# A threshold attention with a maxout feed-forward: the hand-written order of all engines, its PSUM slots and its masks written anew

## The chip, the core and the metric

The kernel runs on one core of one Trainium2 chip. The metric is device time in microseconds (us), from the runs of the whole program. Inputs and output are float32 in the chip's main memory. The engines are named as in the profile: PE (matmul), PEld (its weight loads), DVE (VectorE), ACT (ScalarE), POOL (GpSimd) and SP (SyncE, which here only issues DMAs).

## The reference

```python
# q, k, v: 8 batches x 8 heads x 576 rows x 64;  tau = 0.02
scores = (q @ k.T) / 8
thresh = max(scores, axis=-1) - tau
scores = where(scores >= thresh, scores, -1e9)
attn = exp(scores - max(scores)); attn /= sum(attn) + 1e-9
x = (attn @ v), heads side by side        # 4608 x 512
h = maximum(maximum(x @ w1, x @ w2), x @ w3)   # 512 -> 768
out = h @ w_out                           # 768 -> 512
```

Of each row of scores only the entries within tau of the row's maximum take part in the softmax. The feed-forward works on the rows of one batch, all eight heads together.

## The kernel before, in words

**Attention.** Four heads of a batch make a quad: 16 quads. A quad is worked in 9 chunks, and a chunk in 2 halves, so there are 144 chunks and 288 halves; a half is a score tile of 128 rows x 576 columns (`scores`, line 324). q and k come in as float32, are turned on PE (`transposed`, 293), copied out of PSUM, and q is also copied with its two partition halves exchanged (`swapped`, 277).

**The softmax of a half** has four forms. `MASKED` (line 24) holds one digit for each of the 288 halves and picks the form:

- 0: DVE writes the negated scores from PSUM into a buffer z with the row's extreme (`maximum`, 364); DVE makes the threshold, a small instruction (`threshold`, 375); ACT applies a Prelu to z (`exponents`, 379), then an Exp with a running sum (`numerators`, 388).
- 1: the same DVE pass; ACT applies one Exp to z; DVE then keeps the entries above exp(-tau) and sums them, in one SCALAR_TENSOR_TENSOR that reads z twice (`numerators`). No threshold.
- 2: as 0, but ACT's Prelu reads the scores in PSUM, and no threshold instruction is needed.
- 3: as 1, but ACT's Exp reads the scores in PSUM.

So 0 and 2 take two big ACT instructions and one big DVE one; 1 and 3 take one big ACT and two big DVE. A z buffer is held from the DVE pass until POOL has made the normalised bfloat16 P of that half (`normalized`, 400). There are 9 z buffers (`ZBUFS`, 34); from half 72 on, two more are borrowed (`half_of_z`, 357). When a chunk's P is complete, SP issues a transposing DMA (`turned`, 409), and when all 9 chunks of a quad have landed, two products with v can run (`product`, 415).

**Feed-forward.** For each batch, 18 pieces (6 slices of the hidden width by 3 weights) go through `hid` (490), then two output pieces (`outp`, 526) and a leftover (`ninth`). A piece is cut into two halves (`halves`, 457): the second half adds to the same PSUM as the first from the other half of the rows, so it is gated by a wait on the last matmul of the first half. Batch 7 is split in two parts whose pieces have no halves.

**PSUM.** There are four slots, 0 to 3, of 128 x 1024 float32 each (`bank`, 182). Every PE piece takes the slot whose number is written behind its letter, and has to wait until the piece that used it before has been read out.

**What sets the order.** Nothing is planned at run time. `ORDER` (line 40) is one long text, and the loop at line 789 issues one step for each letter. Each engine runs its own steps in the order in which the text has them (`_Ordered`, 84), and waits for the others by semaphores. The letters, by engine:

- PE: T turn q or k, S scores of a half, O product with v, F first half (or whole) of a feed-forward piece, B its second half, N leftover rows. T, S, O, F and N are followed by the slot.
- DVE: m maximum, s threshold, k masked numerators with sum, r reciprocal of a chunk's sums, c copy of k out of PSUM, w product out of PSUM, v maximum with a feed-forward piece, f the last output.
- ACT: a copy of q out of PSUM, e first exponent step, n Exp with sum, x product out of PSUM, h first of three feed-forward pieces, u output, j leftover rows.
- POOL: p normalise a half, q exchange halves of q, y cast of v, z cast of a weight.
- SP: l a load of q, k or v, g a load of a weight, t transposing DMA, o and i stores. The letter d is the very last output's store, which ACT's queue issues.

The profile puts nearly all instructions on line 93, the helper that every engine's call goes through. They are told apart by tiles: `sc` scores, `z` or `stage` softmax buffers, `P` normalised, `ptq` turned P, `o` product, `xt` feed-forward input, `ph` hidden pieces, `hm`/`hT` their maxima, `po` output in PSUM, `ob` output in SBUF, `tp` turned q and k, `qt`/`kt`/`qs` their copies.

Of the kernel before, what the change touches and what calls it, by code (L numbers as in the profile page):

```python
# [45 lines left out]
nyrrsmyBepT1svS0hpcT2nS3zmaS1erpgsF2mntpsBmnS3yvF1etssT0myeBprS2cnpS3mnS0ympelF2epF3lmBnzslssvS0htBrqmeS2vpn
S1gF0sepmF3teqBmF2erssvpBtnBkphF0eS1vtS3znmF2nrBmqteS1rpvBnS3pmlnF0pmgeS1qsBsrhmS3pevS2npS1mF0npsO3ermpesmO2
zewepgsskBxtT3nF1vS2nklBarS0mlphS3mtepF2sS1rmnyBmetF3pvT0eBpcnS2tzT1nvS0asmzS3temS2qeS1meF0trkpmS3lenpBmnlys
reklpF1umerpskS3upBeoketmS0uS2umpS3tesmS1qeT0myO2nqlrsnlprcO3etqsmepwS0xptS1mnF3psnmS2BlerskpS1thF0meF3pmeBF
2ktnBveBsrS1nvpS0hmyF3emF2npBrssT0eprtvBaF1kS3nqvBeF0myhyS2kyleF3mBelBvnpS2snsS0vptemS1pnF3rmpT2tnBmpeF0scS1  # L50
htBrnmpF3erT2rpvlBasS1pstvnS2pmeF0pS3emtBqnmT2S1hcqS3empF2eS0rsqmtS1epsmBeF3pmnF0stsvBeBknF2klhF1BvelS0nrvpB
emT3pS2arvS0ptnS3mpnO1smtesrkpeF2swnlrpmeT0S1qtescS3epBmnpmnT0trskS3paS1umS0ulqmeS3lmyS1nopS2smelS0rmeS3psmn
O1ypersmqO2etkpemO0lewqxlknpS3tS1keF2momS3lexF0ktT1enkBercpnsBpumN1ertkphkF3jS0rursS1empBnmF2ptS0vpS1smeF3yt
BsnsmBpnvS0pT1hmF2atT3srepS0cF1eprBsmeqF3vnByBynvplS2nsS0plmhS1mteS2mF0nF3mteS1rrspBnmS2pelvBlepF1smT0leqBvl
aS2rkhF3oqnsS0mtS1epmBeqsF2ssmtS0epvBeyF1mnF3vpBesrS0ktphBermS1npT2svO0nytmpncT3eS1wF2nrmS0aBrsmnqF3vnT1pS0c
eBptsF2mhpS1eS3pmteS0qmBeO1spmnkteF3rvnpT0BsskapS2xvS0erS1qmtnS3pmnF2mqlespmeS1rtkBepresmT3puS1cuS0ptmnS3pS2
meyS1lrekpF0tnsmempO3lekteskO2nrsmpeBkpxrnwS1uptS3muS2pnmF0yoeS1mF3lesymBtnS2srkpS1hmBeF0spveF2ertBmpT3nrsvS
1paBlmpnS0tS3qhmF1epsmS2leBymF3tevF0nBknlS1rsvpS2esmqnBF3srmhpS1epS0tmeF2pssBrempBtesvS0ynF1mT3lnpBvF0lhsrcS
2tnT1mBnF3valS2nrBsqmeF0pvS1epS2meBptsmS3eqF1hmT2peBcS3tnskT2O0arkplnmO2lerpvewptS3xkpS1nF2meF0sstreBsmpS3nv
pBnmS1tS2hmT3eF0rmpnF1cBpnBrevptT3S2apvS0qmtS3S1enmqF2esrsqmiepmleS0soykeS1plBnmemtS3ukS0uT1snrlO2cpekynO1me  # L60
ymeF3pwxskteS0keS1BrrnkopmF2pmS0BqeuurtsmF1phS3srnpS2meT0ptBmeS3ykpaN2esvempF0tS1jkpF3ermBeS2ptvnS1pmBnS0rls
hsmpS2elF3mqntS1mpF0nsrBskpeF2lsmBetBpveF1yhvS3lnkS2lesF0mytnBmBerqsS3veF2lpvnF1pBsmT0htBceF3rT2vnpBsaS0pvnF
1qmtS2nBsrnmT0pS3hrcpF2esS1mpteS0rmpS3emBpntF1svqnS0ssBmpeoT2vO3lamtneF1wS0nrlBpmeS3qsrS2hsmS0pnmF1eptS3smeB
pmF2ntS0veS3rsmnpS1BnpO0veytrempS2empS3xsmS1tekF0nsknlT2rmpBelmlpnscS3quS1umyS2eorT0kpeO3tmeyO1ewlepsmF3etka
rknS2qklT0nBmxespcS2eryF0mpF1uskpuBtnS2BhmqF3nsvS0peS2srmtpF1eBmpeF0srvnBptS2hyS3pmeF1lmeBlBevtF3nkT2S0arrvp
BnS2mphS1smpF0ntS3smnpBmeF1lsT2esvlF3nrBrcptBnvpS2eS0qmlhS1tsnprsmT3F2epmS0aptBemF3yevS1oS0nqmBnpsrS2mnF1ptv
S0epmBeS3mthS2skeF0F1snmlBeklO3ersvpnrmByepF0swT2eqtBvnqF3ssrcS1hpiBmpT0S2vaptS1snmS0pnT3mqF2tecT1BarmS3pnS1
vqeS0mF2pesrmnptmS3npT1seS0qctBeymqermpS1eS3mpuF0nmtuskS1eS2klnS3smBesrsepO1upmemO2txrkpukeO3wnkpS0xS2emF3et
rmS1pnBssspmF2hS0rtepS3mnBpmF1etS0veF3mnN2rnpBpjF0evtF2esBkBkhF1nsvS3eBmBevO3hrkS2pwnS1mnF3prmS2eptsF0mnBpsS
1sevyS2terBmpeF3svS1iyepBmoS0yhmtF2ekF3nBsmS1ersBvpnF0pmeF2BvteS1hBmF3rsS0vpeF1rknpBBmnO2vhptO0xrpnS3pwS2trm  # L70
npS0mnF3pmteF1pBeBvtS0rS2vpS3empF1ktkF0kBereskpemBkperumO2uptO3xpN1wtenkO2jrF3pxF1hpF2nvF3tvF1rhF2pvF3pvF1hF
# [758 lines left out]
```

## Time and profile before

| | |
|---|---|
| median of 3 runs | 446.92 us (446.69 to 449.09) |
| profiled execution, span from first to last instruction | 444.8 us |
| what the runs' median has beyond that span | 2.1 us |
| PE busy | 422.4 us (95%) |
| ACT busy | 403.0 us (91%) |
| DVE busy | 392.8 us (88%) |
| POOL busy | 311.9 us (70%) |
| mean DMA traffic | 199 GB/s |

The page gives no time of its own for the profiled execution beside the span, so sums are made against the span, and the 2.1 us are added to compare with the runs. Busy shares are means over stages that differ: a head in which only attention of the first batch can run, a long middle in which attention and feed-forward of earlier batches interleave, and a tail with only the last batch's feed-forward. A busy PE counts matmuls whose ends are modelled, and weight loads have their own row.

### The profile page before, as it was taken

To read this page: it belongs to the slowest core of one execution; us is meant where nothing else is said; L and a number is where in the kernel's file an instruction comes from. 1 tells how busy PE (TensorE), PEld (TensorE's weight loads), DVE (VectorE), ACT (ScalarE), POOL (GpSimd) and SP (SyncE) were. 2 spreads that over 40 slices of the span, in tenths; PEclk is the share of its full clock that TensorE was granted. 3 is DMA by queue.
4 is the path that set the end of the run, shared out by engine and by line. 5 is a ranking of instruction groups with operands and counts; after the bars stand their busy time and mean duration, and the time that the engine had idled before them with its cause. 6 is when DMAs were issued, how large, how long until landed. Compare 5 with 4: busy or idle time off the path is not lost.

```text
span 444.8 us, 14254 instructions
## 1 busy us (share of the span) xinstructions
PE 422.4 (95%) x5188; PEld 320.2 (72%) x5190; DVE 392.8 (88%) x1228; ACT 403.0 (91%) x836; POOL 311.9 (70%) x420
## 2 busy tenths in 40 slices
PE   7767789999999999999999999999999999999996
PEld 6334347787788767787788777788688886787873
DVE  3887999999999999999999999998999998899642
ACT  3999999999999999999999999899999999987632
POOL 2799989997878687696785877676676685457400
PEclk8998999999999999999999999999999999999999
DMA  7999999999999999699899999989999977487633
GB/s 188 275 293 199 291 169 269 235 243 262 229 180 194 212 222 292 125 256 167 143 234 189 230 198 203 209 168 210 208 206 194 244 151 105 83 179 136 145 116 108
DMA packets 213959, 88.50 MB, mean 199 GB/s; under 512 B 189184, under 2 KB 202240, under 8 KB 213888
## 3 DMA queue, kind: packets, MB, share of 16 engines
q1 hardware_dynamic: 213360, 86.96, 95.9%
q8 instruction: 41, 0.67, 0.6%
q10 hardware_dynamic: 528, 0.62, 0.5%
q14 instruction: 30, 0.25, 0.2%
HBM read 35.65 MB, written 9.44 MB: 101 GB/s over the span
## 4 chain that ended last, share of the span: by engine, by line
PE 86%; ACT 5%; DVE 4%; issue 2%; DMA 1%; SPq 0%; DVEq 0%; ACTq 0%
PE ph L93 32%; PE sc L93 32%; PE po L93 10%; PE o L93 9%; ACT z L93 5%; PE tp L93 3%; DVE z L93 3%; DMA qm<-in_q_dram 1%; ACT qt L93 1%; SPq L93 0%; DVE xt L93 0%; DVE hm L93 0%; DVE stage L93 0%; DVE rs L93 0%; ACT ob L93 0%
## 5 line engine op out<-in xcount | busy, mean ns | idle before, releaser
L93 POOL TENSOR_SCALAR P<-z,rs 128x576 bf16<-128x576 f32 x250 | 200.6, 814 | 63.3 <-DVE rs L93 28.1
L93 DVE TENSOR_SCALAR_CACHE_REDUCE z<-sc 128x576 f32<-128x576 f32 x250 | 183.7, 750 | 14.8 <-PE sc L93 10.1
L93 PE MATMUL sc<-kt,qs 64*128 64x256 f32 (+2 forms) x640 | 182.6, 423 | 5.7 <-DVE z L93 2.3
L93 PE MATMUL sc<-kt,qt 64*128 64x320 f32 (+2 forms) x640 | 182.4, 433 | 5.2 <-ACT z L93 3.3
L93 PE MATMUL ph<-xt,w 64*128 64x288 bf16 (+2 forms) x2160 | 170.8, 283 | 0.1
L93 PEld LDWEIGHTS <-w 64*128 64x128 bf16 (+1 forms) x2160 | 130.1, 94 | 28.6 <-issue 4.3
L93 ACT ACTIVATE z<-z 128x576 f32<-128x576 f32 x174 | 117.6, 679 | 0.1
L93 PEld LDWEIGHTS sc<-kt,qs 64*128 64x128 f32 (+1 forms) x640 | 92.4, 180 | 25.7 <-DVE z L93 5.7
L93 ACT ACTIVATE z<-z,th 128x576 f32<-128x576 f32 x143 | 106.2, 769 | 5.0 <-DVE th L93 4.2
L93 PEld LDWEIGHTS sc<-kt,qt 64*128 64x128 f32 (+1 forms) x640 | 91.9, 179 | 19.7 <-ACT z L93 5.9
L93 DVE SCALAR_TENSOR_TENSOR z<-z 128x576 f32<-128x576 f32 x76 | 62.2, 830 | 0.5 <-ACT z L93 0.5
L93 PE MATMUL po<-wo,hT 64*128 64x512 bf16 (+3 forms) x454 | 53.5, 354 | 0.3
L93 POOL COPY qs<-qt 64x640 f32<-64x640 f32 (+3 forms) x66 | 43.0, 652 | 10.8 <-ACT qt L93 7.2
L93 ACT ACTIVATE z<-z,nm 128x576 f32<-128x576 f32 x68 | 50.6, 767 | 0.0
L93 DVE TENSOR_TENSOR hm<-ph,hm 128x576 bf16<-128x576 f32 (+2 forms) x54 | 37.0, 686 | 9.2 <-PE ph L93 8.9
L93 ACT ACTIVATE hm<-ph 128x576 bf16<-128x576 f32 (+2 forms) x54 | 31.8, 589 | 13.4 <-PE ph L93 12.8
L93 POOL TENSOR_SCALAR P<-stage,rs 128x576 bf16<-128x576 f32 x38 | 30.4, 804 | 19.3 <-ACT z L93 5.4
L93 PEld LDWEIGHTS <-hT 64*128 64x128 bf16 (+2 forms) x456 | 30.0, 95 | 16.5 <-issue 2.3
L93 DVE TENSOR_TENSOR hT<-ph,hm 128x576 bf16<-128x576 f32 (+2 forms) x54 | 37.0, 686 | 4.0 <-PE ph L93 2.3
L93 PE MATMUL o<-ptq,vb 128*64 128x64 bf16 (+2 forms) x544 | 39.0, 281 | 0.0
L93 ACT ACTIVATION_READ_ACCUMULATOR z<-z 128x1 f32 x174 | 34.3, 197 | 0.0
L93 PEld LDWEIGHTS <-vb 128*64 128x64 bf16 x544 | 23.3, 111 | 12.8 <-issue 4.9
(45 smaller groups left out, 431.6 us busy)
## 6 DMA issues: line engine op xcount, KB each, us to landing
vm<-in_v_dram SPq DMA_DIRECT2D x32, 256.0 KB, 4.8
qm<-in_q_dram SPq DMA_DIRECT2D x15, 512.0 KB, 5.0
km<-in_k_dram SPq DMA_DIRECT2D x15, 512.0 KB, 5.3
out_dram<-ob SPq DMA_DIRECT2D x14, 512.0 KB, 4.0
stage<-in_moe_w_dram SPq DMA_DIRECT2D x9, 512.0 KB, 5.2
ptq<-P SPq DMA_TRANSPOSE x144, 4.0
vr<-in_v_dram SPq DMA_DIRECT2D x16, 128.0 KB, 3.4
stage<-in_moe_w_out_dram SPq DMA_DIRECT2D x3, 512.0 KB, 4.9
```

Of the source, the lines that this page charges most:

```text
L93: ins = fn(*a, **kw)
```

## The change

Only the two texts change; no function does, and the same pieces are computed.

- **Masks.** Digits 0, 1, 2, 3 stand 169, 78, 33, 8 times before and 155, 91, 27, 15 times after. So 20 halves go from an ACT Exp with sum to the DVE form, and there are 14 threshold instructions fewer. In the first 36 halves, the first batch, the count of 0, 1, 2, 3 goes from 3, 2, 25, 6 to 1, 2, 20, 13.
- **Order.** The steps are all interleaved anew. The sequence of PE pieces differs too, but the first feed-forward piece still follows the 54th S.
- **Slots.** The digits behind the PE letters are new.
- **Halves.** Of the 140 feed-forward pieces cut in two, one had its second half directly behind its first, 73 had one other PE piece between, 41 two, 25 more than two. After, none is direct, 68 have one between, 41 two, 31 more.

The diff, with most lines of the order left out:

```diff
 MASKED = """
-232222322322222222021032222202332122123122122200200111000000000100000000011
-000010111020011000101000000001100001001000010011111100000000100100000000
-110010030111000100010000000001010100001110001011010100110000000000000000
-100101101011000000120000001010000000110011100000001110001000010011111021
+232302322132212223223332232332223223322210201201011000001000001000010011
+000011100100101010010100000000110000110001011111000110200010010000011001
+000000110111100001001000001010100100110000110011300011000100000000100200
+001111100100100011000000001000000110010110111000011010001010100011111111
 """
 ORDER = """
-llllllglllT0laclT1laclzllqqS0qqS1meS2mS3lmlT0enlkS1ylmlT2eamelrnpS3leqlmnyS1qcapS0emtnrcS3pmnT2qmepgrelS1qya
...
-2tvF3vF1hF2voF3vF1ohF2vF3vF1hF2vO3vO1wF2xuuF1oF0hiF3vF1vF0hF3vF1vF0hF3vF1vF0hF3vF1vF0hF3vF1vF0huF3vF1ovF3uoF
-0uoN1fjdi
+llllT1lclaqgqT2lalS1qllcqmS0llS2meS3znmmS1eT0eT2mkS1eaqlcncrslaqmpeS0lmeqpllS3myynS1klmeeS2rnlqT3mS0lknplarm
...
+pvoF2F1hovF0vF3F2hvptvO1O2xwF0iuF2F3F1hF0vF2hvvF3F0oF1vhF2F3vhvF0F1F3vF2hF0vF1F3hvvF2vvF0uF1ouF3foN2dji
 """
```

More of the change, by code (lines that the diff above doesn't have):

```diff
@@ L46 @@
[L46 to L65, printed above, removed]
@@ new lines @@
+2tpeplekS0mmmtnpteS3S1myeeelrmkS2tmnpO0nelwrS3ezmO2S0ksnxetS3pkT1mzlaplS2tmerpnT1S3msT0qS2cprnappmS1peeS0mlm
+ttsrnmneqeknsO2regpS1mS0lwpmglT3zeyO1yxcpptS2rkmS3meS0F1npmrkS2pmnqpsBrF3esT0qhppyBypaveeskF1nF0BnvS2tBmyS3S
+1srsmhtpelzT2mecgF0S3T1naemttBnllpS2vlrqsnmT3csF1teS0BrgpepmS2tmpS3eS0mpsmF2vsF3BS0knF1eBsmzzqgnhrS2nF0Beper
+BtephvlS3spntemvkS2qpqnmF1F0nBsgemS3F2ssrepvntmBtS1BS3zvmrpnmrtleF0hgS1pssnBelmtS3S2pvmpmS1kF0eO3lepyO2mwenz
+T3exBsrkkspvsF1S2BnrmaS0lS3zpehpprmqeF2esmnS1BnF3T0BmgvT1tqecS2S0panpvzmtneeesS1rmemnkyS3S2kF0tppseF1emmktBS
@@ new lines @@
+2srknupstS3urmqrmBppepptuS0mueplS2mS3eS1smmnnqT0O2escerO3lwS1S0rpxkspmteomF2nS3epnS1stF0pmkrtBthF3BmBvepenF2
+S1S0esvF3yrpeoBmthmneBkslevF1F2pS0kT3rlmBBrlsaS0hvksF3ptpF1qmpBnpevlBS0nS2vF3nsmS1pBtF0ymseT2meneS1sBhqynsrc
+eyF3T2mprllvBarS1S2lF0vS3mspT1pneBmnetS2qmpS3hnS0cF1mrS2smtenpeyqF3epsmBpsmF0nvF2kBrBepBhvF1estkvlS0mBteevT3
+aS2mptnS0rS1O3ppnlprmT0nF2tmswT3eS1lecnyqaptsykkrppS0smenS3BS1mS0mperetustrmS3qpupeS1mtS2mS0mkmS3pO1nrO2epmk
+slemeO0T3elssywnxteexkeS1rekncnF2prqF0BpmlpS1pS3ktkumyouBelS2mmrhqS1F3espeemN0jrptBykF2nvslS0eS1ppprF3nmBlmB
@@ new lines @@
+nS0T1vhF3msT2kpS0ncaqeF1BptBmF0svnS2vrpepmS3qsepBtlnS1msmhS2F0etF1mrkesstS3nS2elBrBnmppF3vT0lpmslepavBkS2mrr
+S0mF1hesppS3BF2mnF0BqenovytsBeT1vS3cF2lS1hmtpS0nmBemsprO3T0vwS1eF2senmekrqapltpS0F3T1eenpymqcBvstrBS0S1nmhpt
+qltF2spmsS3nlS0O1BmpemssF3keetnvxynT0aByekS2rvnmpsrS1meS0ntppS3F2mT1nremeptS0S3slBtpmpS0emnrucpuS3pemmtS1eks
+S2repqqkemmF0O3O1nekrpxBtesrtwS1ukpkppusS3oemmS2S0smF1tF3BrenmlsyBF0S2hpkvepeS1rmnBF3yT2pnBpsvaS0mkS1hemmrnp
+nesF2eS3nBlmlpS1yF0trmF3BvssBkS1trethpS2vpF3sS0nmpmqtmreS1BspF2F0lseeBnmS1BvT3qlveelpmcS2heF1pT0sptmkBsnaF3l
@@ new lines @@
+S2vrmBvF0nptS1S2tneresnlmpmirS3pmnBF1pthT2cpeBepsqvsT0S3kemtnaO2kellnrO1F0wlkqpS3xsBrS1epmeF3myspS2nvrsnBphS
+1romS0T3F2mppmF1eencyBvBlqsvT3eS0apS2emS3S1T0ptnmetrF2qntsnpmemkS3esmS1cmtBpqS0emS3trsyputO1kwukeeneO2mF1epx
+kenrS3S2rpF0sBenllummpBkppsS2S3ukmryF1hmstrneoT0BaqptS2S3evtF0emprypS1tmN2tBmskF1ejnkvelnS2mS3pmpssspBF0hter
+epS2S3pS1mlrBF2mF3psvBneqmnBtlerpF1S0hnnvkeS2mtF3tsmBS0vpF2msBsesnvnBrhpeT0sF1ernycqF3S2BnmyvBT0F2vS1ptpaeT0
+mlqptesBS3cS1phnmmrpS0sS2nysmrF3emF1pBeBevS2snmvO3ewT2ekF1qseS0S3nBpampmS2snS0rphlpnerF3sS1mretF2pelmBinS0mp
```

22 lines of the change are left out of this document (11 added, 11 removed).

## The prediction

> **What bounds the kernel now.** I read the page's busy shares first, then a table of windows cut at three places: the first score piece (7.48), the start of feed-forward (73.5) and the last score piece (406.5). Columns: length, then busy us of PE, PEld, DVE, ACT, POOL, the granted clock, DMA share, GB/s.
>
> ```profile
> PE 422.4 (95%) x5188; PEld 320.2 (72%) x5190; DVE 392.8 (88%) x1228; ACT 403.0 (91%) x836; POOL 311.9 (70%) x420
> 7.48:30.90 23.42, 17.09 (x151) 9.95 (x146) 18.65 (x53) 20.83 (x47) 17.78 (x27) 0.93 1.14 282
> 30.90:51.40 20.50, 16.05 (x108) 9.10 (x108) 16.67 (x54) 20.07 (x45) 19.59 (x27) 0.83 1.12 238
> 51.40:73.50 22.10, 18.96 (x204) 10.98 (x206) 21.94 (x66) 21.85 (x46) 19.42 (x23) 1.00 1.09 219
> 73.50:406.50 333.00, 331.74 (x4350) 261.13 (x4348) 314.55 (x1001) 323.84 (x668) 246.31 (x331) 1.00 1.01 199
> 406.50:444.80 38.30, 33.88 (x334) 24.72 (x334) 19.61 (x51) 14.70 (x33) 8.07 (x10) 0.99 0.47 126
> ```
>
> By the page's shares three engines are about equal. The windows separate them. In the middle PE is idle for 1.26 of 333.00 us. In the head it is short of work; ACT is the full engine (20.07 of 20.50 in the second stretch), joined by DVE in the third (21.94 of 22.10).
>
> Is the busy PE of the middle at its pace? The chain that ended last, in order of time (start, us, what), says so:
>
> ```profile
> 10.80 2.04 ACT z L93 x4
> 19.84 3.22 ACT z L93 x7
> 37.66 4.08 ACT z L93 x8
> 53.34 1.59 DVE z L93 x5
> 61.01 1.59 DVE z L93 x5
> 69.46 2.59 PE o L93 x40
> 202.39 0.97 PE ph L93 x16
> 397.86 0.98 PE ph L93 x16
> ```
>
> Two feed-forward halves (16 matmuls) take 0.97 us at 202 and 0.98 at 398: one pace, and it is PE's. The first lines show the head: ACT leads until past 40, then DVE, and at 69.46 come the products that close the first batch. So the end is the start of feed-forward plus PE work that the change leaves as it is. What can move is that start, and whether the new order keeps PE fed behind it.
>
> **The change part by part.** *Masks and order in the head.* Feed-forward starts after the last product's two copies into its input (`xt`), one on DVE, one on ACT:
>
> ```profile
> 8.87 0.76 DVE L93 TENSOR_SCALAR_CACHE_REDUCE z<-sc 128x576 f32<-128x576 f32 x1 [0.47 <-PE sc L93]
> 71.16 0.75 DVE L93 CAST xt<-o 128x576 bf16<-128x576 f32 x1
> 71.83 1.19 DVE L93 SCALAR_TENSOR_TENSOR z<-z 128x576 f32<-128x576 f32 x1
> 72.94 0.08 DVE L93 DVE_READ_ACCUMULATOR z<-z 128x1 f32 x1
> 71.04 0.68 ACT L93 ACTIVATE z<-z 128x576 f32<-128x576 f32 x1
> 71.71 0.67 ACT L93 ACTIVATE z<-z 128x576 f32<-128x576 f32 x1
> 72.37 0.64 ACT L93 ACTIVATE xt<-o 128x576 bf16<-128x576 f32 x1
> 73.06 0.67 PE L93 MATMUL ph<-xt,w 64*128 64x288 bf16 x8
> ```
>
> From the order text I counted what stands on each engine ahead of its copy. ACT: 49 e and 37 n before, 49 e and 28 n after, the rest equal. An Exp with its sum takes 0.67 from start to start (71.04, 71.71), so ACT could reach its copy 9 x 0.67 = 6.0 us earlier. DVE: 7 k more (11 to 18), and 2 m, 1 c, 1 r and 3 s fewer; the m and c are only moved behind. The head's groups:
>
> ```profile
> L93 DVE TENSOR_SCALAR_CACHE_REDUCE z<-sc 128x576 f32<-128x576 f32 x53 | 38.8, 751 | 6.5 <-PE sc L93 4.9 <-POOL P L93 1.2
> L93 DVE SCALAR_TENSOR_TENSOR z<-z 128x576 f32<-128x576 f32 x12 | 11.5, 962 | 0.5 <-ACT z L93 0.5
> L93 POOL TENSOR_SCALAR P<-z,rs 128x576 bf16<-128x576 f32 x46 | 37.2, 823 | 3.7 <-DVE rs L93 2.6
> ```
>
> A k lasts 962 ns here; the one of 1.19 above lets its successor start after 1.11, so an average one counts 0.88: 7 x 0.88 = 6.2. Off go two m at 0.67 (751 less the same 0.08), 1.3, a copy c, some 0.6, and about 0.3 for r and s: DVE gets 4.0 us more. Its idle time in the head is 4.77 + 3.83 + 0.16 = 8.8 by the windows; some 1.4 of that lie ahead of its first m (8.87), so 7.4 can go. The two ends: feed-forward starts 4.0 later if all this idle time stays, 3.4 earlier if all goes (ACT's 6.0 is out of reach, DVE then being the full one). Why was DVE idle? Waits in the head:
>
> ```profile
> PEld sc L93 <- ACT z L93: 10.0, 19, 1.0
> PEld sc L93 <- DVE z L93: 5.9, 7, 1.8
> PEld tp L93 <- ACT z L93: 4.7, 4, 2.5
> PE sc L93 <- ACT z L93: 4.0, 9, 0.7
> PE tp L93 <- ACT z L93: 2.9, 2, 2.1
> ```
>
> DVE waited for scores (4.9 of 6.5 above), and PE, to write them, for ACT to read out a slot: 10.0 + 4.7 + 4.0 + 2.9 = 21.6 against 5.9 for DVE's own part. That ACT has 6.0 less queued. The nearest row for a head in which DVE is the full engine is the third stretch, 0.16 idle in 22.10; at that rate some 0.4 of the 7.4 stays. I take -3.0.
>
> *What the extra k do to POOL.* P and k last 823 and 962 ns in the head, so they disturb each other; the 0.88 has k's share in it. POOL is busy for 56.8 of 66.0 us of the head. The Trainium skill, "SBUF — State Buffer", section "Who interferes with whom", says that a VectorE instruction with two SBUF inputs, as k is, and a GpSimd one that reads SBUF exclude each other, and the second waits for the whole of the first. By that rule seven more k could hold POOL for up to 6.2 us, and if all of it reached the copies the sum would be 450.5. POOL's 9.2 idle us take it up here, so I cost it at nothing; rival three is the case without that cover.
>
> *Queues of the head.* Ahead of the 18th transposition, the first batch's last, SP issues 35 loads of q, k, v and 5 of weights before, 33 and 4 after.
>
> ```profile
> 56.25 10.68 SPq L93 DMA_TRANSPOSE ptq<-P  x5
> 57.57 2.90 POOL L93 TENSOR_SCALAR P<-z,rs 128x576 bf16<-128x576 f32 x4 [2.30 <-DVE rs L93]
> k<-in_k_dram SPq DMA_DIRECT2D x7, 128.0 KB, 3.3
> qm<-in_q_dram SPq DMA_DIRECT2D x15, 512.0 KB, 5.0
> stage<-in_moe_w_dram SPq DMA_DIRECT2D x9, 512.0 KB, 5.2
> ```
>
> The batch's last P ends at 60.47, but SP issues without a pause until 66.93, the products starting at 69.46: transpositions queue. Three transfers fewer are 128 + 512 + 512 KB, at 219 GB/s (third stretch) 5.3 us. So the landing moves by 0 to -5.3, which covers the -3.0; I add nothing. In the new order the last quad's products stand behind 49 and 51 score pieces (52 before): were the landing late, the score pieces behind them would queue. POOL's cast of the first weight goes behind four q exchanges instead of ahead: 0, as ACT is full from 10.80 either way.
>
> *Slots and halves in the middle.* PE is full there, so each wait counts. One pair of halves ran back to back and no longer does: at most one half, 0.49. The other distances hardly move. I take 0; the ends are PE's 1.26 of idle time as a gain, and rival one as a loss. The Trainium skill, "Perfetto Trace Analysis", section "Identifying the Most-Contended Engine", calls matmul busy time a bad measure and uses that of weight loads, here 261.13 of 333.00, or 78%. By it PE would not be full, the busiest of the others would set the middle (ACT's 323.84 now, DVE's 325.2 after, from rival one), and the sum would be 1.3 more, 445.6. The even 0.97 and 0.98 above speak against it.
>
> *Tail.* In ACT's queue the leftover rows' copy (j) stood ahead of the last output's store (d); after, d stands ahead.
>
> ```profile
> 440.53 0.39 ACT L93 ACTIVATE ob<-po 128x256 f32<-128x256 f32 x1 [1.43 <-PE po L93]
> 440.54 1.29 ACTq L93 DMA_DIRECT2D out_dram<-ob  x2
> ```
>
> Two issues take 1.29. With d first, j starts some 0.65 later and the store that follows it about 0.4 later: +0.4, or 0 if d lands last anyway.
>
> *Sum.* 444.8 - 3.0 + 0.4 = 442.2 of span; the runs' median stands 2.1 above the span: 444.3.
>
> **The rivals.** *One, the other side: DVE becomes the middle's bound.*
>
> ```profile
> L93 DVE SCALAR_TENSOR_TENSOR z<-z 128x576 f32<-128x576 f32 x59 | 47.1, 809 | 0.0
> ```
>
> 13 of the 20 new k fall behind the head: 13 x 0.73 (809 less 0.08) = 9.5, plus the 1.9 moved there, less 11 s at 0.07: +10.6, DVE 325.2 of 333.00. For it: DVE's 18.45 idle us shrink to 7.8 if PE is to keep its pace. Against: ACT kept up at 323.84, and loses 11 n, 7.4. If the idle time stays, the middle grows by 10.6: 454.9. It is slower by over 0.5% once more than 12.7 of the 18.45 stay (10.6 - 5.75 = 4.85 lost, 2.6 of it paid for by the head).
>
> *Two: all goes through.* Head -3.4, the 1.26 gone, no loss in the tail: 444.8 - 4.7 + 2.1 = 442.2. For it: fewer transfers and 6.0 less on ACT leave slack in the head.
>
> *Three: the head keeps its length,* since z buffers or POOL hold it. When DVE reaches a chunk's r, it has issued 3.8 m beyond that chunk on average over the first 27 chunks, after 4.5, of nine buffers. A buffer held 0.7 m longer at 66.0 / 53 = 1.25 us per m eats 0.9 of the 3.0 in the mean, and all of it where the chain is tight: 446.9 + 0.4 = 447.3. POOL can do the same: should each of the seven k stop a P for its length (6.2) at a time when the copies wait for it, 450.5. Against: POOL idles in the head, 2.6 of the 3.7 ahead of P for a late r, so it is mostly not the one waited for.
>
> **How the numbers follow.** A measurement of this kernel can tell about 0.5%, 2.2 us, from no change, so faster means below 444.7, slower above 449.2. Forecast 0.50 (own range 442.5 to 446.0; 0.36 faster, 0.14 the same, as 444.3 lies near the border). Rival two 0.10, faster. Rival three, 447.3 to 450.5, 0.14 (0.10 same, 0.04 slower). The middle at DVE's 325.2, 445.6, lies in the forecast's own range. Rival one 0.26 (0.25 slower, 0.01 same). Together 0.46, 0.25, 0.29. The range runs from 439.5, a little under rival two for what waits inside the middle could still give, to 453.0, most of rival one.
>
> **What would show it.** Right: the first `ph` matmul near 70.0 instead of 73.06; DVE idle under 3 us between first score and feed-forward; ACT busy about 13 us lower in all (20 x 0.67), DVE about 14 higher (20 x 0.75 less 14 x 0.07); PE idle in the middle still near 1 us and its halves in pairs at 0.97; 38.7 us from the last score to the end. Wrong: DVE's m waiting for P (buffers), PE's scores waiting for DVE's z in the middle, or products waiting for `ptq` with score pieces behind them.

## The result

The changed kernel takes 466.12 us (median of 4 runs, 465.85 to 468.1), the kernel before 447.05 beside it (446.69 to 449.09): a ratio of 1.043, with a 95% interval from 1.040 to 1.047. The prediction was 444.3, in a range of 439.5 to 453.0, so it has the wrong sign and the time lies far outside. The profiled execution after has a span of 464.2, against 444.8.

The first part of the page after (in its rows the helper is line 92, as the text of the order is one line shorter):

```profile
PE 426.6 (92%) x5188; PEld 319.1 (69%) x5190; DVE 408.9 (88%) x1254; ACT 394.2 (85%) x796; POOL 325.6 (70%) x420
```

ACT has 9 us less (13 were reckoned) and DVE 16 more (14). To see where the time went I cut both spans at the same work: first score piece, first feed-forward piece, score piece 108, the last score piece (287, counting from 0). First before, then after; the columns are those of the prediction's table.

```profile
7.48:73.06 65.58, 51.65 (x454) 29.63 (x449) 56.82 (x171) 62.30 (x136) 56.35 (x75) 0.92 1.12 247
73.06:146.80 73.74, 73.68 (x982) 60.52 (x981) 71.02 (x228) 73.53 (x153) 63.52 (x85) 1.00 1.13 225
146.80:406.50 259.70, 258.50 (x3377) 201.02 (x3376) 243.96 (x774) 250.75 (x516) 183.23 (x247) 1.00 0.97 191
```

```profile
6.96:73.44 66.48, 49.13 (x453) 31.19 (x451) 60.46 (x180) 58.85 (x119) 59.12 (x73) 0.92 1.08 236
73.44:155.70 82.26, 76.00 (x982) 59.57 (x980) 74.24 (x236) 74.15 (x152) 65.07 (x86) 0.98 1.00 217
155.70:418.40 262.70, 260.20 (x3379) 198.33 (x3376) 250.61 (x778) 245.64 (x497) 189.41 (x246) 1.00 0.95 187
418.40:464.20 45.80, 36.33 (x335) 25.38 (x334) 22.21 (x55) 13.79 (x29) 10.73 (x11) 0.90 0.45 105
```

The matmul counts agree by stage (982, 3,377 and 3,379, 334 and 335), so the stages hold the same PE work. Feed-forward starts at 73.44 instead of 73.06: 0.4 later, where 3.0 sooner was forecast. The stretch behind it, 982 matmuls, takes 8.5 more: PE is idle for 6.3 of 82.26 us, before for 0.06 of 73.74, and it is busy for 2.3 longer with the same matmuls (76.00, before 73.68). The long rest of the middle takes 3.0 more, the tail 7.5 more (38.30 before). Together that is the 19.4 by which the spans differ.

**The head.** The third of the four products, the copies of the last two and the first `ph` after, then two of its waits and two of its groups (columns as in the prediction):

```profile
67.32 1.12 PE L92 MATMUL o<-ptq,vb 128*64 128x512 bf16 x14 [1.15 <-DMA ptq<-P]
70.28 0.76 DVE L92 CAST xt<-o 128x576 bf16<-128x576 f32 x1
71.88 0.65 ACT L92 ACTIVATE xt<-o 128x576 bf16<-128x576 f32 x1 [1.38 <-PE o L92]
73.44 0.66 PE L92 MATMUL ph<-xt,w 64*128 64x288 bf16 x8
...
PEld sc L92 <- ACT z L92: 10.1, 15, 1.5
ACT z L92 <- DVE z L92: 5.2, 10, 0.9
...
L92 POOL TENSOR_SCALAR P<-z,rs 128x576 bf16<-128x576 f32 x44 | 37.3, 860 | 1.2
L92 DVE SCALAR_TENSOR_TENSOR z<-z 128x576 f32<-128x576 f32 x19 | 17.1, 909 | 0.0
```

Before, ACT waited less for DVE:

```profile
ACT z L93 <- DVE z L93: 2.4, 3, 1.3
```

DVE's copy is ready earlier, and ACT's now waits 1.38 for the last product instead of standing behind its own row. But DVE keeps 6.0 of its 8.8 idle us (66.48 less 60.46), and ACT, 3.5 less busy, waits 5.2 for DVE's z instead of 2.4. PE waits as long as before for ACT to read out a slot (10.1, before 10.0; the four rows that the prediction added up to 21.6 come to 21.9 after).

The batch's last transposition tells how far the start could move. Its P ends later (62.60, before 60.47). Fewer loads stand ahead of it on SP, and it goes out 1.30 us behind its P instead of 4.95, and lands at 67.19 instead of 68.90: 1.7 sooner. The third product waits 1.15 us for this landing, and the fourth stands behind two score pieces and a T and starts at 70.42; before, the two run back to back from 69.39.

**Behind the head.** Rows after of the first late load: SP's issues and the T that reads it; then POOL's cast of a weight that came late too, and what follows from it on DVE, on PE and in the clock. Then the same load and T before:

```profile
71.51 5.36 SPq L92 DMA_TRANSPOSE ptq<-P  x2
76.93 0.63 SPq L92 DMA_DIRECT2D km<-in_k_dram  x1
81.72 0.46 PE L92 MATMUL tp<-identf,km 64*128 64x64 f32 x8 [1.53 <-DMA km<-in_k_dram]
92.09 1.04 POOL L92 CAST w<-stage 128x1024 bf16<-128x1024 f32 x1 [2.68 <-DMA stage<-in_moe_w_dram]
94.78 0.76 DVE L92 TENSOR_SCALAR_CACHE_REDUCE z<-sc 128x576 f32<-128x576 f32 x1 [2.52 <-POOL P L92]
95.60 0.53 PE L92 MATMUL sc<-kt,qs 64*128 64x320 f32 x1 [2.01 <-DVE z L92]
...
96.57:99.99 3.42, 3.42 (x29) 2.68 (x27) 2.69 (x11) 2.26 (x5) 3.17 (x5) 0.50 1.09 217
```

```profile
67.74 0.47 SPq L93 DMA_DIRECT2D km<-in_k_dram  x1
83.34 0.51 PE L93 MATMUL tp<-identf,km 64*128 64x64 f32 x8
```

Before, k of quad 4 is issued 15.6 us ahead of its T; after, 4.8, behind two transpositions that hold SP for 5.4, and T waits. q of quads 5 and 6 and k of quad 15 are nearly as tight: issued 6.2, 5.3 and 6.4 us ahead of their T, which wait 0.88, 1.53 and 1.26.

The weight works through a chain. POOL stands 2.68 us at the cast of a weight that SP issued only at 87.71 and that landed at 92.03. The P behind it come late, so no z buffer is free and DVE's m waits 2.52; score piece 67 waits 2.01 for the slot that DVE has not read out; and behind that wait the granted clock is 0.50 for 3.4 us. That one wait and the three of T are 6.0 of the 6.3 us in which PE is idle; the half clock is, by an estimate from its length, 1.7 of the 2.3 us that PE is busy longer. The chain can be followed through other runs below: where these weight loads stay, PE's wait at score piece 67 follows POOL's at that cast (0.39 for 0.34 in a_q18v, 0.66 for 0.73 in a_tail, 1.52 for 1.60 in a_tmask4, 2.09 for 2.16 in a_q18; in a_all, with 0.69 on POOL, PE does not wait); where they too are put ahead (a_loads, a_early, a_late18), POOL does not wait there and PE waits 0.4.

**The tail.** SP's last transposition and stores after, the product that waits, and the clock behind that wait; then SP before:

```profile
432.95 1.25 SPq L92 DMA_DIRECT2D out_dram<-ob  x2
434.29 2.51 SPq L92 DMA_TRANSPOSE ptq<-P  x1
...
440.34 1.06 PE L92 MATMUL o<-ptq,vb 128*64 128x256 bf16 x7 [4.76 <-DMA ptq<-P]
...
440.30:444.00 3.70, 3.44 (x41) 2.85 (x43) 0.49 (x1) 0.44 (x1) 0.00 (x0) 0.50 0.00 0
```

```profile
402.87 17.28 SPq L93 DMA_TRANSPOSE ptq<-P  x8
420.21 1.26 SPq L93 DMA_DIRECT2D out_dram<-ob  x2
```

Before, the eight last transpositions go out before the stores. After, two output stores stand ahead of the last one; it is issued late, lands 6.0 us after its issue, and PE waits 4.76 and then works at a granted clock of 0.50.

### The profile page after: what moved, and what is told of

Read it like the earlier page. It is cut to its first block, busy times and chain, and to the rows that moved or that the text cites. A ratio compares the mean times of both kernels' runs of the same rounds, so it can differ in the third digit from the quotient of the medians.

```text
span 464.2 us, 14246 instructions
## 1 busy us (share of the span) xinstructions
PE 426.6 (92%) x5188; PEld 319.1 (69%) x5190; DVE 408.9 (88%) x1254; ACT 394.2 (85%) x796; POOL 325.6 (70%) x420
## 4 chain that ended last, share of the span: by engine, by line
PE 71%; POOL 7%; DMA 7%; DVE 7%; issue 4%; SPq 2%; ACT 1%; POOLq 0%; ACTq 0%; DVEq 0%
PE sc L92 26%; PE ph L92 25%; PE po L92 9%; PE o L92 8%; POOL P L92 4%; DVE z L92 4%; PE tp L92 3%; DMA ptq<-P 3%; DMA qm<-in_q_dram 2%; SPq L92 2%; POOL qs L92 2%; DMA km<-in_k_dram 1%; DMA stage<-in_moe_w_dram 1%; DVE kt L92 1%; POOL vr L92 0%
## 5 line engine op out<-in xcount | busy, mean ns | idle before, releaser
L92 PE MATMUL sc<-kt,qt 64*128 64x320 f32 (+2 forms) x640 | 179.2, 430 | 6.9 <-DVE kt L92 2.8
L92 PE MATMUL sc<-kt,qs 64*128 64x256 f32 (+2 forms) x640 | 178.0, 419 | 7.7 <-POOL qs L92 2.6
L92 ACT ACTIVATE z<-z 128x576 f32<-128x576 f32 x155 | 104.4, 675 | 0.2
L92 ACT ACTIVATE z<-z,th 128x576 f32<-128x576 f32 x130 | 96.8, 768 | 3.4 <-DVE th L92 2.8
L92 DVE SCALAR_TENSOR_TENSOR z<-z 128x576 f32<-128x576 f32 x95 | 80.6, 857 | 0.0
L92 POOL COPY qs<-qt 64x640 f32<-64x640 f32 (+3 forms) x66 | 48.6, 736 | 21.3 <-ACT qt L92 17.7
L92 ACT ACTIVATE z<-z,nm 128x576 f32<-128x576 f32 x81 | 60.4, 768 | 0.3 <-DVE z L92 0.3
L92 PE MATMUL o<-ptq,vb 128*64 128x512 bf16 (+2 forms) x544 | 41.4, 287 | 7.2 <-DMA ptq<-P 5.9
L92 POOL TENSOR_SCALAR P<-stage,rs 128x576 bf16<-128x576 f32 x38 | 33.5, 887 | 12.7 <-DVE rs L92 7.2
L92 ACT ACTIVATE z<-sc,nm 128x576 f32<-128x576 f32 x39 | 28.1, 740 | 5.4 <-DVE z L92 5.2
```

What stands on the lines that cost most here:

```text
L92: ins = fn(*a, **kw)
```

## The experiments

Names that begin with b are the kernel before with one thing changed, those with a the changed kernel. A caution on sizes: runs with the same head as the changed kernel started feed-forward anywhere from 73.4 to 77.3 in their profiles (before's order 73.1 to 73.7), so differences of 2 us between a-kernels are read from stages, not from times. The stages have a spread too: the stretch to score piece 108 took 79.9 to 82.8 in the six kernels whose loads and masks there are the changed kernel's (after, a_tail, a_tmask4, a_tmask4o, a_y, a_c). The table gives the median time and, from each trace, the start of feed-forward, the two stretches of the middle, and the tail.

| run | time | feed-forward starts | to score piece 108 | to the last one | to the end |
|---|---|---|---|---|---|
| before | 447.05 | 73.1 | 73.7 | 259.7 | 38.3 |
| after | 466.12 | 73.4 | 82.3 | 262.7 | 45.8 |
| b_loads | 452.55 | 73.7 | 80.7 | 260.0 | 37.8 |
| b_hmask | 457.79 | 82.8 | 74.1 | 260.2 | 38.5 |
| ab27 | 455.08 | 80.7 | 75.3 | 259.7 | 38.1 |
| b_y | 451.07 | 77.8 | 74.8 | 259.7 | 37.9 |
| b_tmask4 | 446.84 | 73.3 | 73.7 | 259.7 | 38.3 |
| a_loads | 465.98 | 77.0 | 80.6 | 261.0 | 45.7 |
| a_early | 470.47 | 77.8 | 79.6 | 264.5 | 45.2 |
| a_late18 | 464.37 | 73.6 | 80.1 | 261.9 | 45.9 |
| a_q18 | 464.77 | 75.7 | 80.2 | 261.2 | 45.8 |
| a_q18v | 462.06 | 75.0 | 77.4 | 261.6 | 46.4 |
| a_q18m144 | 481.71 | 74.7 | 82.5 | 277.7 | 45.1 |
| a_tail | 460.22 | 77.3 | 79.9 | 263.3 | 38.3 |
| a_tmask4 | 461.81 | 74.8 | 81.3 | 262.1 | 41.1 |
| a_tmask4o | 462.24 | 77.1 | 82.8 | 261.9 | 40.2 |
| a_best | 456.58 | 74.7 | 79.6 | 263.5 | 37.8 |
| a_all | 455.93 | 73.8 | 82.3 | 263.7 | 38.1 |
| a_y | 467.4 | 74.7 | 81.7 | 263.4 | 46.6 |
| a_c | 468.89 | 75.4 | 82.5 | 262.2 | 46.1 |

Two things stand out. With before's order behind it, the middle takes the same 259.7 and 74 to 75 however late it starts; and no a-kernel gets near 73.7.

### Late loads: b_loads and a_loads

The edit moves loads alone in SP's row. In numbers of transpositions ahead of each:

```diff
 b_loads           q3  k3  q4  k4  q5  q6  k6  q15
-before             8   8  13  18  25  36  38  116
+                  13  14  18  21  30  42  42  119
 a_loads
-after             13  14  18  21  30  42  42  119
+                  11  11  13  18  25  36  38  116
```

The rows left over of q and k (quads 4 and 6), the v loads between them and weight loads from w6 on (counted from w0) go along, as far as buffers allow.

> The kernel before, with those same loads of q, k, v and weights put as far behind the transpositions as in the changed kernel; masks, order of all compute engines and slots are before's. Late loads: 447.0 grows by 5 to 8 us, to 452 to 455, with T pieces that wait for q and k between 75 and 145. Masks: unchanged, 446.5 to 447.5.

> The changed kernel, in which SP issues the loads of q, k, v for quads 3 to 6 and 15 and five weights as far ahead of the transpositions as the kernel before did, or as far as the buffers allow (q of quad 5 ahead of 25 transpositions instead of 30, q of quad 6 ahead of 36 instead of 42). Nothing else moves. Theory *late loads* (SP's queue hands the loads out behind transpositions that wait for P, and PE's T pieces and POOL's weight cast wait for them): the stalls at 81.7 (1.75), 95.6 (2.26), 109.5 (1.03), 141.3 (1.77) and 368.7 (1.5) go, 8.3 us in all, and the time falls from 466.1 to about 458. Rival *masks* (13 more k hold up DVE and POOL in the first third): the stalls move elsewhere and the time stays within 465 to 467.

b_loads took 452.55, a ratio of 1.011 (1.007 to 1.014) to before: 5.4 us lost by the places of loads alone. The stretch of 982 matmuls grows from 73.7 to 80.7 (in an execution 1.5 us above the median), with two T waits (window, then PE's rows):

```profile
73.70:154.40 80.70, 75.81 (x983) 62.04 (x982) 71.42 (x228) 74.34 (x153) 63.85 (x85) 0.98 1.04 212
...
105.63 0.46 PE L93 MATMUL tp<-identf,qm 64*128 64x64 f32 x8 [1.78 <-DVE rs L93]
137.34 0.46 PE L93 MATMUL tp<-identf,qm 64*128 64x64 f32 x8 [3.05 <-DMA qm<-in_q_dram]
```

So late loads are a cause, shown in before's own order. (The releaser named at 105.63 is the last seen by the profile; T there reads the q that was moved, which landed at 105.50.) But a_loads gave nothing back: its stretch of 80.6 is within what the six kernels with unchanged loads took (79.9 to 82.8), and feed-forward started at 77.0. The late-loads theory expected 458 there and missed by 8. In its trace the T wait of quad 5 (1.45 us) and one of a score piece (1.36) are put down to DVE, not to a load.

### How far it can be undone: a_late18, a_early, a_q18

```diff
 a_late18: only loads behind the 18th transposition, weights too
+k4 21->18  q5 30->25  q6 42->36  k6 42->38  q15 119->116  w6 21->18  w7 24->22
 a_early: these, and ahead of the 18th
+v2 5->2  q3 13->8  k3 14->8  v3 15->10  q4 18->13  (weights ahead of the 18th stay)
 a_q18: as a_late18, but all weight loads stay
```

> The changed kernel; only loads that stand behind its 18th transposition are moved, to where the kernel before has them: k of quad 4 from 21 to 18 transpositions ahead of it, q of quad 5 from 30 to 25, q and k of quad 6 from 42 to 36 and 38, two weights, v, and q of quad 15. Up to 68 us nothing differs. If these loads' places make the waits of T and of the weight cast behind the head: 4 to 6.5 us off 466.1, that is 459.5 to 462, and no T stall above 0.6 left at quads 4, 5 and 6. If the first moving of loads gave nothing since the waits come from elsewhere: 465 to 467.

> As the former, and also the loads of quads 2 to 4 that the changed kernel issues between its 5th and 18th transpositions are moved ahead to before's places (q and k of quad 3 from 13 and 14 to 8, v from 15 to 10, the leftover rows of quad 4 from 16 and 18 to 10 and 11, its q from 18 to 13); weights stay. If SP's row of loads between the last transpositions of the first batch holds the products up (the landing of the 17th and 18th at 71 to 75): feed-forward starts 2 to 4 us sooner than in the changed kernel (73.4 there, 77.3 in the run with the other tail) and the time is 455 to 459. If transpositions wait for P in that stretch: start unchanged, and the time is that of the run with late loads moved alone.

> The changed kernel with only the loads of q, k and v behind the 18th transposition moved to before's places (k of quad 4, q of 5, q and k of 6, q of 15, the v between them); the weight loads stay where the changed kernel has them. In the run that moved the weight loads too, the 19th transposition was issued 8.8 us after its P, against 2.9 in the changed kernel: SP stood at a weight load whose stage buffer POOL had not yet emptied. If the loads' places cost what PE waited for at quads 4, 5, 6 and 15: that delay is back near 3 and the time is 459 to 462. If the transpositions' row on SP is the deeper cause, and any load put ahead only shifts it: 463.5 to 466.

a_late18 gained 1.7 us, a_early lost 4.4, a_q18 gained 1.4: all below or against what the late-loads theory gave. Their waits say why. First a_late18, SP's own waits from 60 to 110; then two of a_early's head:

```profile
SPq L92 <- POOL w L92: 3.1, 1, 3.1
```

```profile
DVE z L92 <- POOL P L92: 6.3, 6, 2.6
POOL P L92 <- DMA ptq<-P: 4.2, 2, 3.9
```

In a_late18 SP stands at a weight load whose stage buffer POOL has not emptied, with transpositions behind it: the 19th goes out 8.8 us after its P. In a_early the loads themselves make the transpositions late; then P's buffers are not free, POOL waits (4.2), z's buffers are not free, and DVE waits (6.3). A load put ahead on SP is a transposition put back. The T waits of 1.53 at quad 4 and 1.5 at quad 6 are gone in both kernels, and yet the stretch took 80.1 and 80.2, where six runs with unchanged loads there took 79.9 to 82.8: most of the wait was handed on.

### SP's row or DVE: a_q18v and a_q18m144

```diff
 a_q18v: a_q18 and
-            sync.dma_start(out=L["vm"]...
+            (scalar if 3 <= g <= 6 else sync).dma_start(out=L["vm"]...
 a_q18m144: a_q18 and before's digits for halves 54 to 143 (24 k instead of 31)
```

> As the former, and the v loads of quads 3 to 6, eight issues, go out from ACT's queue instead of SP's. SP is rid of about 8 x 0.6 = 5 us of issuing between 55 and 140. If SP's row (transpositions issued 5 to 10 us after their P, so that P's buffers and then z's buffers come free late, and DVE waits for POOL's P) sets the pace from 73 to 147: 2 to 5 us less than the former. If DVE does: the same as the former within 1 us, or up to 2 more for ACT's issues.

> As the first of these, with the kernel before's masks for halves 54 to 143, at the same places in the order: 24 k instead of 31 there, so 7 x 0.75 = 5 us less on DVE and 7 x 0.67 = 4.7 more on ACT. If DVE bounds that stretch (rival one of the prediction): 4 to 6 us less than the first. If SP's row does: within 1 us of it; ACT's more could also cost, up to 3.

a_q18v took 462.06, 2.7 less than a_q18; the stretch fell from 80.2 to 77.4 (its window first, a_q18's below):

```profile
75.00:152.40 77.40, 75.50 (x982) 57.71 (x980) 74.43 (x236) 74.23 (x152) 63.74 (x85) 1.00 1.04 224
```

```profile
75.70:155.90 80.20, 76.78 (x983) 58.60 (x981) 73.89 (x236) 74.38 (x152) 65.14 (x86) 0.98 1.07 219
```

Eight issues taken off SP, with the same bytes, are worth 2.7 us, and the stretch is below that of every other a-kernel: SP's row is one of the bounds there. The chain of the late weight shows how. POOL's wait at its cast falls from 2.16 to 0.34, PE's at score piece 67 from 2.09 to 0.39, and the 3.4 us at half clock behind it are gone (0.98 and 1.00 in the windows). The Trainium skill, "DMA: Bandwidth & Descriptors", section "Rules for kernel authors", says that spreading DMAs over issuing engines buys no bandwidth and only saves issue time; the trace agrees (219 and 224 GB/s), and here the issue time was what counted.

Before's digits did not help but cost 17 us, 16.5 of them behind score piece 108 (277.7 against 261.2). They are seven k fewer by count, but 37 of the 90 halves change their form. Two of its waits there; in a_q18 the second is 0.9, and PE waits for none of ACT's copies of q:

```profile
PE sc L93 <- ACT qt L93: 3.4, 2, 2.9
ACT z L93 <- DVE th L93: 7.3, 7, 2.2
```

The n stood where the k had stood, and a threshold that a digit 0 needs stood just ahead of its e; so ACT waits for DVE, and PE for the copies that queue behind on ACT. Fewer k at given places is no relief: masks and order belong together. Whether fewer k in an order made for them would help, this run can't tell.

### The masks of the head: b_hmask, ab27

```diff
 b_hmask: MASKED, halves 0 to 53
-232222322322222222021032222202332122123122122200200111
+232302322132212223223332232332223223322210201201011000
 ab27: the changed kernel's order, slots and masks up to score piece 27, before's from there
```

> The kernel before with the changed kernel's masks for the halves 0 to 53 alone: seven more k on DVE and nine fewer n on ACT in the head, put at the places where the old letter stood; order, slots and loads are before's. If the extra k hold up POOL or DVE (rivals three and one of the prediction, in the head): feed-forward starts 2 to 6 us later than 73.1 and the time is 449 to 453. If ACT was the bound and the masks alone relieve it: start near 70 and 444. If the order must go with them: within 446 to 448.

> The changed kernel up to its score piece 27, from there before's order, slots and masks. The changed kernel is ahead by 3.8 at that piece (38.9 against 42.7) and has lost all of it nine pieces later. If its order and masks between pieces 27 and 54 lose the lead: feed-forward starts near 70 and the time is 443 to 445, ahead of the kernel before. If the lead is borrowed (work of POOL, SP and DVE put off): it is lost again under before's order, and the time is 446 to 449.

b_hmask took 457.79, 11.2 more than the 446.59 of before beside it, beyond what was expected: feed-forward starts at 82.8. Its window to that point, and one of its waits (before, ACT waits 2.4 for DVE's z):

```profile
7.20:82.80 75.60, 54.97 (x455) 33.29 (x453) 63.01 (x187) 59.39 (x122) 61.02 (x76) 0.84 1.06 240
...
ACT z L93 <- DVE z L93: 11.4, 14, 1.8
```

ACT has less to do, as the prediction reckoned, and waits 11.4 us for DVE instead; DVE is idle for 12.6 of 75.60. The new masks cost the head 9.7 us in before's order. They are seven k more by count, but 25 of the 54 halves change their form, so the 9.7 is the price of masks that do not fit the order, not of seven instructions. The new order wins nearly all of it back, and no more.

ab27 started feed-forward at 80.7. It does not show what became of the lead of 3.8 us, because the lead is not there: score piece 27 starts at 46.04 (38.91 after, 42.69 before).

```profile
46.04 0.80 PE L93 MATMUL sc<-kt,qt 64*64 64x320 f32 x2 [4.08 <-ACT z L93]
```

Where the two texts meet, the steps that the new order had put off by then (transpositions, exchanges of q, casts, loads: `gzglttlqtzllt`) stand in one clump. That fits work put off that has to be made up. But already at piece 24, ahead of that place, it stood at 37.9 (35.4 after), and whether the lead is borrowed stays open.

### Which row takes the lead: a_y, b_y, a_c

```diff
 a_y, b_y: the casts of v, quads 0 to 3
-        pool.tensor_copy(out=L["vb"], in_=L["vm"])
+        scalar.activation(out=L["vb"], in_=L["vm"], func=AF.Copy)
 a_c: order, behind score piece 31
-S1ppmenqpmT2eckqenkt
+S1ppeT2cmnqpmekqenkt
```

> The changed kernel with the casts of v (128 x 1024, 1.04 us and more each) of quads 0 to 3 made by ACT instead of POOL, at the same places in the order. In the changed kernel POOL is busy for 38.9 of 46.4 us from 5 to 51.4, and the lead of 3.8 us goes there in waits for POOL's qs (2.8 at 30.8) and for DVE's kt behind an m that waited 0.9 for POOL's P. If POOL sets the head (rival three of the prediction): the lead at score piece 36 is 1 to 3 us instead of 0, feed-forward starts at 70.5 to 72.5 and the time falls by 1 to 3. If DVE or SP's row sets it, or ACT takes the loss: no lead at piece 36 and a time within 1.5 us of 466.1, or above it.

> The kernel before with the same four casts on ACT. There ACT is the full engine of the head (41.3 of 46.4) and POOL has time: if that reading is right, feed-forward starts 2 to 4 us later than 73.1 and the time is 449 to 451. If POOL sets the head here too: the start is earlier than 73.1 and the time below 446.5.

> The changed kernel with one instruction of the head moved: DVE's copy of kt for quad 2 (the one that score piece 32 waits 2.66 us for) goes ahead of the two m that stand before it on DVE, of which the first waits 0.9 us for POOL's P. All other engines' orders are the same. If DVE's in-order row loses the lead between pieces 27 and 36: piece 32 comes 1.4 to 1.7 us sooner, the lead at piece 36 is that much, and the time falls by up to 1.7. If other rows are as full: part of it is gone again by feed-forward (73.4), and the time is within 1.5 of 466.1.

a_y took 467.4 (no gain), b_y 451.07 (4.0 lost, the upper end of what was expected). Head windows of a_y and b_y:

```profile
6.90:74.70 67.80, 49.79 (x456) 31.71 (x454) 60.63 (x180) 60.87 (x122) 55.91 (x71) 0.92 1.08 233
```

```profile
7.60:77.80 70.20, 55.36 (x452) 30.94 (x448) 56.07 (x171) 65.36 (x139) 53.40 (x72) 0.85 1.07 243
```

In the head before, ACT is the full engine (65.36 of 70.20 in b_y), so that reading of the prediction holds. In the changed kernel POOL's casts are not what holds it. Nor is the kt copy alone. The wait of score piece 32 for it fell as expected (after first, a_c below), but the piece came only 0.2 sooner, as this execution was 1.4 behind at piece 27. Score piece 36 then waited for ACT, and the start of feed-forward was no sooner:

```profile
47.36 0.79 PE L92 MATMUL sc<-kt,qt 64*128 64x256 f32 x1 [2.52 <-DVE kt L92]
```

```profile
47.13 0.48 PE L92 MATMUL sc<-kt,qt 64*128 64x256 f32 x1 [0.79 <-DVE kt L92]
52.11 0.48 PE L92 MATMUL sc<-kt,qs 64*128 64x256 f32 x1 [0.80 <-ACT z L92]
```

DVE, ACT and POOL are busy for 60.46, 58.85 and 59.12 of 66.48 us, each in its own order, and here a wait taken away brought up the next. With a spread of 4 us in the start, these two runs could not have shown a gain of 1 or 2. No single row was found that owns the head.

### The tail: a_tail, a_tmask4, b_tmask4, a_tmask4o

```diff
 a_tail: from score piece 264 before's order, slots and masks
 a_tmask4: MASKED, last four digits
-1111
+1021
 b_tmask4: the same four in before
-1021
+1111
 a_tmask4o: a_tmask4, and the stores o behind the last transposition
-pvoF2F1hovF0vF3F2hvptv
+pvF2F1hvF0vF3F2hvptoov
```

> The changed kernel up to its score piece 264; from there the rest of the order, the slots and the masks of the halves not begun are those of the kernel before. Theory *tail* (the last 24 halves' masks and order make the last P, the last transposition and so the last products late): the stretch from the last score piece to the end falls from 45.8 to about 38.5 and the time from 466.1 to about 458.8. Rival (the tail is long because the middle hands its work over late): the stretch stays above 44 and the time at 465 to 467.

> The changed kernel with two digits of MASKED put back to before's, halves 284 to 287 from 1111 to 1021: two k fewer on DVE among the last, two n more on ACT at the same places, one s. If DVE's k at the very end sets the last P: 1.5 to 3 us off, 463 to 464.6. If SP's order there (stores of the output ahead of the last transposition) sets it: 0 to 0.5 off.

> The kernel before with the changed kernel's digits for halves 284 to 287, 1111 instead of 1021: two more k on DVE among the last, two n fewer on ACT, at the same places. The mirror of the run that took these two k out of the changed kernel and gained 4.3 us. If two k there cost the same in any order: 450 to 451.5. If before's order has room for them, since its last transposition lands well ahead of the products that read it: 447 to 448.5.

> The changed kernel with the two digits of the last halves (as in the run with them alone, 461.8) and with the two output stores that SP issues ahead of the last transposition put behind it. If these stores hold the last transposition (issued 1.3 us after its P and landed 5.9 later, against 0.0 and 3.2 in the kernel before): the stretch from the last score piece to the end falls from 41.1 to 38.3 to 39.5 and the time to 459 to 460.5. If the last P sets it: 461.3 to 462.3.

The tail's windows of a_tail and a_tmask4, and SP in a_tmask4 (the tails of the others stand in the table):

```profile
420.50:458.80 38.30, 33.86 (x334) 24.73 (x332) 19.60 (x51) 14.71 (x33) 8.06 (x10) 1.00 0.47 124
```

```profile
418.20:459.30 41.10, 34.54 (x334) 24.14 (x334) 20.43 (x52) 15.02 (x33) 9.23 (x11) 0.98 0.48 117
...
431.37 1.25 SPq L92 DMA_DIRECT2D out_dram<-ob  x2
433.34 1.74 SPq L92 DMA_TRANSPOSE ptq<-P  x1
```

The tail's order and masks cost 7.5 us: with before's it takes 38.3 again. Two k fewer give 4.7 of that, but not as the first theory had it: the last P ends at the same time (433.3 against 433.0). What moves is the chunk ahead of it, whose P ends at 429.9 instead of 431.6. So the two stores behind that chunk's transposition are issued 1.6 sooner and are out of the way: the last transposition goes out when its P is ready and lands 2.8 sooner. PE then waits 0.66 instead of 4.76, and the mean clock of the tail is 0.98 instead of 0.90. Putting the stores behind it gives another 0.9 of tail; its time (462.24) can't be told from 461.81 and misses what was expected, with feed-forward starting 2.3 later in its profile. The 1.9 that are left to 38.3 belong to the rest of the order there. In before, where the stores come last anyway, the same two k cost nothing: 446.84, a ratio of 0.9985 (0.9964 to 1.0006).

### Do the causes add up: a_best, a_all

```diff
 a_best: a_q18, and a_tail's end
 a_all: a_best, v loads as in a_q18v, casts as in a_y
```

> The first of these up to its score piece 264, from there before's order, slots and masks (as in the run with the other tail). If the two causes add up: 5.5 to 7.5 us less than the first, 453 to 456; the stretch from the last score piece to the end is 38.3 again. Left over against 447 are then 6 to 9 us that neither the late loads nor the tail explains.

> The changed kernel with all that gave something: q, k and v loads behind the 18th transposition at before's places, the v loads of quads 3 to 6 on ACT's queue, the v casts of quads 0 to 3 on ACT, and before's order, slots and masks from score piece 264. If the terms add (0 to 3 for the casts, 1.3 for the loads' places, 2.7 for the queue, 8 for the tail): 451 to 454. Faster than the kernel before would need 446.0 or less, which none of these terms leads to.

a_best took 456.58, 8.2 less than a_q18: the two causes add up (tail 37.8). a_all took 455.93: its tail adds up too (38.1), the rest does not. In its trace the stretch of 982 matmuls is back at 82.3, and ACT stands still there for 4.05 us:

```profile
110.26 0.61 ACTq L92 DMA_DIRECT2D vm<-in_v_dram  x1
110.98 0.78 ACT L92 ACTIVATE z<-z,th 128x576 f32<-128x576 f32 x1 [4.05 <-DMA stage<-in_moe_w_out_dram]
```

ACT's last work ends at 106.92, and what stands next in its row is one of the v loads that were moved to it. It goes out only at 110.26, just behind the landing that the profile names. In a_q18v the same load goes out 0.4 us after the work ahead of it. So a load on a computing engine's queue can stop that engine; why this one waited for a load of the output weight is not shown. The profiled execution took 459.65, the other three 455.4 to 456.1, so the median may hold less of this. None beats the kernel before.

## Why the prediction was wrong

The span was put at 442.2 and came out at 464.2, 22.0 more: 3.4 of that in the head (-3.0 forecast, +0.4 measured), 11.5 in the middle (0 forecast) and 7.1 in the tail (+0.4 forecast, 7.5 measured).

**Masks and order in the head, -3.0: failed, +0.4.** The count was right (ACT lighter, DVE heavier). The step that failed is that all but 0.4 of DVE's 7.4 idle us would go: its work grew by 3.6 (4.0 were reckoned), its idle time shrank by only 2.7, and the 0.9 between them, less a first score piece 0.5 sooner, is the +0.4. The row that set the rate, the head's third stretch, is one where the engines had been lined up. The reading of the waits misled too. It set 21.6 us of PE's and PEld's waits for ACT against 5.9 for DVE, which is one row of several: the same view of before has 3.5, 2.6, 2.0, 1.6 and 1.0 more for DVE's z and kt, 16.6 in all. PE was held by both, and ACT's part did not shrink (21.9 after). b_hmask showed the size of what was left out: in an order not made for them the new masks cost 9.7 us, since ACT, ahead of its work, waits for DVE in turn. The forecast treated idle time as free for the taking; it was the slack between rows that wait for each other.

**Extra k against POOL, cost nothing: not refuted.** k's mean went from 962 to 909 ns, that of P from 823 to 860, and POOL was 2.8 busier. Taking three casts of 1.2 off POOL in the head gave nothing (a_y), so POOL's time was not the one missing. The rule that the prediction cited (the Trainium skill, "SBUF — State Buffer", "Who interferes with whom") would have allowed up to 6.2; the trace shows at most those 2.8.

**Queues of the head, "I add nothing": failed, about +7 in the middle.** In the head, the landing was to move by 0 to -5.3 and so to cover the -3.0; it moved by -1.7, as the last P came 2.1 later, and would have capped the gain there. The larger part lies behind. The step counted the loads ahead of the 18th transposition, saw three fewer, and took that for slack. It did not ask where they had gone: behind transpositions that wait for P, and the first pieces to need them are T's in the middle. b_loads prices this at 5.4 us of time and 7.0 of the stretch. That trade is all SP's row has: loads put ahead again made transpositions late, and P's and z's buffers after them, which the prediction had listed among its wrong signs.

**Slots and halves in the middle, 0: not separated.** They were not tried by themselves. What can be theirs is part of the 3.0 us that the long rest of the middle lost, and part of the stretch ahead of it: there, at a clock of 1.00, PE was busy for 75.0 to 76.3 us with the changed order's pieces and for 73.7 to 74.4 with before's.

**Tail, +0.4: far too small.** The step named is there: d goes out ahead of j, and j's store follows it (461.03 after, ACT's queue):

```profile
459.81 0.63 ACTq L92 DMA_DIRECT2D out_dram<-ob  x1
460.62 0.38 ACT L92 ACTIVATE ob<-po 128x256 f32<-128x256 f32 x1 [2.18 <-PE po L92]
461.03 0.51 ACTq L92 DMA_DIRECT2D out_dram<-ob  x1
```

But it looked at the last two letters only. The last transposition behind two stores, and the masks that set when these go, cost 5.6 of the 7.5 (45.8 to 40.2 in a_tmask4o); the rest of the tail's order has the other 1.9.

**The rivals.** Rival one had the right sign and the wrong mechanism. DVE is not full in the stretch that lost most (74.24 of 82.26). Taking k away there made it worse, but at places made for other masks, so that run speaks neither for nor against it. Rival three was right that the head would keep its length. Its buffers hold DVE in a_early (6.3); in the changed kernel's head they hold it for 1.2, as before, and no one row does. Behind the head they hold it for 2.52 at 94.78, through the late weight. So two of the signs of being wrong that the prediction named, m waiting for P and scores in the middle waiting for z, are there once behind the head, and SP's row stands behind both.

**What stays open.** Of the 8.5 us lost between the start of feed-forward and score piece 108, loads and SP's issues account for 2.5 to 5.4 (77.4 in a_q18v, against 79.9 to 82.8 in the six runs without them). For the 3.7 that a_q18v still lacks to before (1.8 of PE's idle time, 1.8 of PE being busy longer), for what holds the changed head at 73.4 and for its spread of 4 us, no experiment singles out a cause.

## What to carry to other kernels

When an order is rewritten, list for every load how many waiting instructions of its queue now stand ahead of it, against the time from its landing to its first use: the row of a full queue is a budget, and what is put ahead on it is paid by what falls behind. Idle time of an engine in a stage where three are nearly full is not a reserve; price a shift of work between them by the waits of the next engine, not by the sum of durations. A stage in which the bounding engine is idle for 0.06 of 73.74 us can only lose by a new order, so the chance of a loss there has to be weighed with that in view.

## What the runs showed of the hardware

- A transposing DMA (128 x 1152, bfloat16) holds SP for 1.2 us and lands 3.2 after its issue when little else moves (the last one before). Beside two 512 KB stores it held 2.5 and landed after 6.0 (the last one after). Among loads, from 60 to 90 us, one held 4.6 in a_q18 and one landed after 9.3 in a_q18v.
- A wait can cost PE more than its length. After 4.76 us without data the granted clock was 0.50 for the next 3.7 us, and 7 matmuls took 1.06 us; in a_tmask4, after a wait of 0.66, the same 7 took 0.62. Shorter waits did it too: 3.4 us at 0.50 followed the 2.01 us at 95.60 in the changed kernel, the 2.09 at 97.30 in a_q18 and the 3.05 at 137.34 in b_loads. A wait of 2.02 in a_tmask4 (at 141.62) left the clock at 1.00, so at some 2 us it can go either way.
- The Trainium skill, "TensorE: Matmul & The Clock Gate", section "HAM oscillation — how this bites in real kernels", states that PE falls to half its clock when idle for more than some 3.4 us. The waits of 4.76 and 0.66 agree; those of 2.01, 2.09 and 3.05 do not, and here the measurement decides: waits of 2 to 3 us have to be counted as ones that can halve the clock.
- A load on ACT's queue can stop ACT: 4.05 us in a_all, with the next instruction behind a v load that went out late.
- The profile's named releaser can be off where several waits end together: T's wait in b_loads at 105.63 is put down to a DVE instruction, though only loads were changed and the q that it reads landed at 105.50.
